# Attention outputs turned in 32 by 32 blocks by VectorE, and an output stage without TensorE transposes

## The chip, the cores and the metric

The kernel runs on one core of one Trainium2 chip. A core has a matrix engine (TensorE, in the profile PE for its matmuls and PEld for its weight loads), three engines that work on vectors (VectorE or DVE, ScalarE or ACT, GpSimd or POOL), and SyncE (SP), which in this kernel does nothing but issue DMAs, all in one queue and in the order of the program. Each engine works through its own instructions in order and waits on semaphores for the others. The metric is the device time of one execution in microseconds, lower is better; the number used is the median of three runs.

## The reference, cut to what matters

Two independent parts whose results stand side by side in the output:

```python
S, D, H, Dh, N, L = 2048, 576, 32, 18, 4, 512      # N segments of L rows

# part A: Infini-attention
q, k, v = (x @ w for w in (wq, wk, wv))            # split into 32 heads of 18
for s in range(N):
    p = softmax(q_s @ k_s.T * scale + causal_mask)  # within the segment
    a_dot = p @ v_s
    a_mem = (phi(q_s) @ M) / (phi(q_s) @ z + 1e-6)  # memory of the earlier segments
    o_s = g * a_mem + (1 - g) * a_dot               # g = sigmoid(beta), one per head
    M += phi(k_s).T @ v_s;  z += phi(k_s).sum(rows)
a = concat(o_s).reshape(S, D) @ wo

# part B: FNet mixing
b = dft_seq_re @ (x_b @ dft_hid_re.T) - dft_seq_im @ (x_b @ dft_hid_im.T)
return concatenate([a, b], axis=-1)                # S x 1152, float32
```

The change concerns the way of `o_s` to the product with `wo`. That product needs the attention output with the features (576 = 32 heads x 18) on the partitions, while attention produces it with the rows (positions) on the partitions, so that somewhere a transpose is needed.

## The kernel before, in words

The dense products run in three parts: each operand is split into a high part (rounded to the matmul's format) and a low rest, and hi*lo + hi*hi + lo*hi are added in PSUM.

**Stage 1, projections** (about 0 to 235 us). For each of the four segments, q, k and v are computed and written to DRAM (`qd`, `kd`, `vd`), and for segments 1 to 3 the memory term, already multiplied by g, is written by `lookup` as row tiles `amd[t]` of 128 x 576, t = 0..15 (L364, L365).

**Stage 2, attention woven into the dense FNet products** (about 235 to 950 us). Two generators run side by side. `dense()` gives the FNet matmuls in small pieces (`hidden`, `sequence`, L510 and L555 to L560). `attention()` (L826) walks over 64 steps p of two heads each, plus four steps in which the pipeline empties. Each step has eight slots with planned lengths (`SLOTS`); after each slot the main loop (L894) puts in as many dense matmuls as keep the two in proportion. The matmuls of attention are short and wait for other engines, those of `dense` wait for little, so that TensorE always has something to do. The order in which each engine gets its instructions is exactly the order in which this Python code runs. `later(n, f)` puts a call n slots later.

A group G is four heads; it takes two steps, 2G and 2G + 1, and there are 32 of them, eight per segment. In a step, `s_fill` (slots 0, 2, 3) computes scores of the even head for the row minima, which VectorE takes with a custom instruction (L691); `f_fill` (slots 4, 5, 6) does the same for the odd head of two steps earlier, whose exponentials ScalarE then takes (L714). Both take turns at two PSUM banks with the tag `s`: the matmul of `f_fill` kind 1 in slot 4 writes the bank whose scores of `s_fill` kind 1, slot 2, VectorE must have read. `t_lo` (L784) and `f_split_lo` (L725) are splits of the probabilities, partly on VectorE and partly on GpSimd; the odd head's probabilities are turned by a DMA transpose (L730). `pv` (L801, L802) multiplies with v.

Four steps after a step began its heads, in slot 7, `pv_out` (L804) normalises their output: a reciprocal, a product with 1 - g, a reduction over three parts (L816) and a product (L817) into the tile `og`, 128 partitions x 4 x 4 x 18, two buffers. After the second half of a group, `og` is written to `od[s][g8]` in DRAM (L820), with rows on the partitions and 4 x 72 features and row tiles in a row.

`y` (four buffers of 128 x 576) holds results of the dense products; in the second half of `dense` its tiles come back from DRAM (`y_load`), VectorE subtracts the PSUM result (L579), and the tile goes to the output's right half.

**Stage 3, output** (about 950 us to the end). For each of 16 row tiles, `o_load` fetches the eight group pieces of 128 x 72 and, for segments 1 to 3, the memory tile `amd[t]`; `o_join` adds the two on VectorE (L631) and copies the last 64 features twice (`otail`, L633); `o_transpose` turns five 128 x 128 blocks on TensorE (L644), and ScalarE and VectorE split the result from PSUM (L57, L649, L650). The main loop (L914) then runs two chains of 14 matmuls with the weights `wo` (28 per tile, L925 through the helper at L79), ScalarE takes the result out of PSUM (L926), and one DMA writes the tile (L930; in the last tile one for each half, L928). The loads for tile t + 2 are issued when tile t is transposed. The work for tile 0 starts about 3 us before the last dense matmul.

Of the kernel before, what the change touches and what calls it, by code (L numbers as in the profile page):

```python
# [38 lines left out]
def infini_attention_and_fnet(ctx: ExitStack, tc: tile.TileContext, xT, wqk, w8, wv, wo, beta, xtT, cT, hT, out):  # L39
# [10 lines left out]
    vd = [dram.tile([P, 4, 8, 220], BF16, name=f"vd{s}") for s in range(NSEG)]  # L50
    amd = [dram.tile([P, D], F32, name=f"amd{t}") for t in range(NT)]
    yd = [dram.tile([P, D], F32, name=f"yd{t}") for t in range(NT)]
    od = [dram.tile([8, P, 4, 72], F32, name=f"od{s}") for s in range(NSEG)]

# [28 lines left out]
    def later(n, fn, *a):  # L83
        due.setdefault(clock[0] + n, []).append((fn, a))
# [256 lines left out]
    def lookup(s, j):  # L341
# [22 lines left out]
        pool.tensor_tensor(am, nd[:, :, :DH], w.to_broadcast([P, H, DH]), OP.mult)  # L364
        later(1, dma, amd[4 * s + j], am.rearrange("p h d -> p (h d)"))  # L365
        yield
# [47 lines left out]

    CAUSAL, NEGM, MB = [], [], []

# [83 lines left out]
    def bank(name, shape, dtype, tag):  # L500
        turns[tag] ^= 1
        return ps.tile(shape, dtype, name=name, tag=f"{tag}{turns[tag]}", bufs=1)
# [34 lines left out]
    def y_load(tt):  # L537
        if tt < NT:
            Y[tt] = sb.tile([P, D], F32, name="y", bufs=4)
            dma(Y[tt], yd[tt])  # L540
# [26 lines left out]
    def sequence(ri, tt):  # L567
        if ri:
            y_load(tt + 1)
            y = Y.pop(tt)  # L570
        else:
            y = sb.tile([P, D], F32, name="y", bufs=4)

# [38 lines left out]
    O, O3, OT, WO, WORAW = {}, [], {}, [], []  # L612

    def o_load(t):
        if t >= NT:
            return
        s, j = divmod(t, 4)
        a = O3[0].tile([P, D], F32, name="o", bufs=3) if O3 else sb.tile([P, D], F32, name="raw", tag="raw", bufs=3)
        dma(a.rearrange("p (g c) -> p g c", g=8), od[s][:, :, j, :].rearrange("g p c -> p g c"))
        m = None  # L620
        if s:
            m = O3[0].tile([P, D], F32, name="oam", bufs=3)
            dma(m, amd[t])
        O[t] = a, m

    def o_join(t):
        if t >= NT:
            return
        a, m = O[t]
        if m is not None:  # L630
            dve.tensor_tensor(a, a, m, OP.add)  # L631
        tail = O3[0].tile([P, P], F32, name="otail", bufs=2)
        dve.tensor_copy(tail.rearrange("p (r c) -> p r c", r=2), a[:, None, 512:].to_broadcast([P, 2, 64]))  # L633
        O[t] = a, tail

    def o_transpose(t):
        if t >= NT:
            return
        o_load(t + 2)
        a, tail = O.pop(t)  # L640
        o = bank("ot", [P, 4, P], F32, "s")
        e = bank("ot1", [P, P], F32, "t")
        for c in range(5):
            pe.transpose(o[:, c] if c < 4 else e, a[:, c * P:(c + 1) * P] if c < 4 else tail, ident)  # L644
        hi = O3[0].tile([P, 4, P], F32R, name="oth", bufs=2)
        lo = O3[0].tile([P, 4, P], F32R, name="otl", bufs=2)
        tl = O3[0].tile([P, P], F32R, name="ott", bufs=2)
        split(hi, lo, o)
        act.activation(tl, e, AF.Copy)  # L649
        dve.tensor_tensor(tl[64:], e[64:], tl[64:].bitcast(F32), OP.subtract)  # L650
        OT[t] = hi, lo, tl
        o_join(t + 1)

# [15 lines left out]
    sa = p2a.enter_context(tc.tile_pool(name="sb2a", bufs=1, reuse_waits="tile"))  # L669
    PT, OG, PV = {}, {}, {}  # L670

# [132 lines left out]
    def pv_out(n2):  # L804
        G, hh = divmod(n2, 2)
        s, g8 = divmod(G, 8)
        o = PV.pop(n2)
        if hh == 0:
            OG[G] = sa.tile([P, 4, 4, DH], F32, name="og", bufs=2)
        h0 = 4 * g8 + 2 * hh  # L810
# [5 lines left out]
        dve.tensor_reduce(a, o[:, :, :, :54].rearrange("p h i (c d) -> p (h i) d c", c=3), axis=AX, op=OP.add)  # L816
        dve.tensor_tensor(OG[G][:, :, 2 * hh:2 * hh + 2, :].rearrange("p i h d -> p h i d"),  # L817
                          a.rearrange("p (h i) d -> p h i d", h=2), w.to_broadcast([P, 2, 4, DH]), OP.mult)
        if hh == 1:
            later(4, dma, od[s][g8], OG.pop(G).rearrange("p i h d -> p i (h d)"))  # L820

# [4 lines left out]
    def attention():  # L826
        for p in range(NP + V_LAG):
# [8 lines left out]
            if p < 2:  # L836
                stacks(sa, p + 2)
            if p == 0:
                value_load(0)
                stack_load(1)  # L840
            if p % 2 == 0:
                later(39, value_load, p // 2 + 1)
            if p == NP + 1:
                o_load(0)
                o_load(1)
# [59 lines left out]
    for t in d:  # L905
        tick()
        td += t or 0.0
        if 0 in O and td > total_d - 3000.0:
            o_join(0)
            o_transpose(0)  # L910
    while due:
        tick()

    for t in range(NT):  # L914
        o_transpose(t + 1)
        hi, lo, tl = OT.pop(t)
        y = O3[0].tile([P, D], F32, name="y3", bufs=2)
        for h in range(2):
# [7 lines left out]
            act.activation(y[:, cs], o, AF.Copy)  # L926
            if t == NT - 1:
                dma(out[t * P:, cs], y[:, cs])  # L928
        if t < NT - 1:
            dma(out[t * P:(t + 1) * P, :D], y)  # L930


_INS = ("xT", "wqk", "w8", "wv", "wo", "beta", "xtT", "cT", "hT")


# [28 lines left out]
```

## Time and profile before

| what | value |
|---|---|
| median of 3 runs | 1020.28 us (1017.42 to 1022.33) |
| the profiled execution: its time, its span | 1024.34 us, 1022.6 us |
| TensorE busy, matmuls | 1007.7 us (99%) |
| VectorE busy | 727.8 us (71%) |
| ScalarE busy | 711.4 us (70%) |
| GpSimd busy | 626.1 us (61%) |
| DMA | 208.39 MB, 297757 packets, mean 204 GB/s |

The profile is that of one execution. Busy shares are means over stages with different limits, so the stages have to be looked at by themselves. A row of a group of instructions gives the line, engine and operation, the tiles (written <- read), the shapes and the count, then after the bar the busy time in all and the mean of one in ns, then how long the engine stood idle just before them and what ended that. In the chain of work that ended last, each row has a start, a length, and the instruction. The timeline has start, length, engine, line, operation and tiles; an idle time before an instruction stands in brackets at the end of its row.

### The profile page before, as it was taken

The page shows a single profiled execution, that of the slowest core. Times are in us where ns is not written, and L with a number is a line of the kernel's source. Part 1 is how long each engine was busy: PE and PEld are TensorE (multiplying, and loading weights), DVE is VectorE, ACT ScalarE, POOL GpSimd, SP SyncE. Part 2 cuts the span into 40 slices and gives each one's busy share as a digit, 9 for nine tenths or more (in the row PEclk, how much of TensorE's full clock was granted, in tenths as well). Part 3 has the DMA queues.
Part 4 walks back from the last instruction along what each step waited for, and adds up shares of the span by engine and source line. Part 5 has one row for each costly group of instructions (what it writes and reads, how often), then busy time and mean ns, then how long its engine had stood idle before and what let it go on. Part 6 is the DMA issues. An engine that isn't in the chain of part 4 may idle for free.

```text
span 1022.6 us, 25516 instructions
## 1 busy us (share of the span) xinstructions
PE 1007.7 (99%) x9464; PEld 944.0 (92%) x9464; DVE 727.8 (71%) x1903; ACT 711.4 (70%) x1654; POOL 626.1 (61%) x668
## 2 busy tenths in 40 slices
PE   9999999989999999999999999999999999999998
PEld 8989989879999999999999999998999999999998
DVE  6645555555577777877888788887889888885442
ACT  7657475544687878787878788886768787875333
POOL 3557584775667676766775777666666676775000
PEclk9999999999999999999999999999999999999999
DMA  7538465677477989898898898688999999887574
GB/s 258 178 102 272 149 178 216 202 255 228 109 179 196 220 227 206 218 221 218 213 261 209 225 200 178 167 216 216 218 214 217 241 212 240 237 175 176 158 210 138
DMA packets 297757, 208.39 MB, mean 204 GB/s; under 512 B 208672, under 2 KB 250784, under 8 KB 297632
## 3 DMA queue, kind: packets, MB, share of 16 engines
q1 hardware_dynamic: 297632, 206.76, 77.4%
q8 instruction: 74, 1.21, 0.5%
q14 instruction: 51, 0.42, 0.1%
HBM read 120.80 MB, written 57.93 MB: 175 GB/s over the span
## 4 chain that ended last, share of the span: by engine, by line
PE 84%; DMA 4%; DVE 4%; ACT 3%; POOL 3%; issue 2%; POOLq 0%; SPq 0%; DVEq 0%; ACTq 0%
PE d L510 38%; PE s L685 7%; PE d L79 6%; PE pv L801 4%; PE qk L231 4%; PE qk L79 3%; PE d L555 3%; PE d L556 3%; PE d L557 3%; PE v L79 3%; PE pv L802 2%; PE t L759 1%; POOL p L268 1%; DMA amd<-am 1%; PE m L324 1%
## 5 line engine op out<-in xcount | busy, mean ns | idle before, releaser
L691 DVE CUSTOM_DVE_ANT_0 s<-s,causal 128x128 f32<-128x128 f32 (+3 forms) x512 | 250.4, 499 | 92.1 <-PE s L685 84.0
L403 POOL TENSOR_TENSOR clo<-craw,chi 128x512 fp32r<-128x512 f32 x158 | 212.0, 1342 | 103.1 <-ACT chi L398 71.7
L510 PE MATMUL d<-wide,chi 128*128 128x288 f32 x1408 | 266.7, 306 | 0.0
L510 PEld LDWEIGHTS d<-wide,chi 128*128 128x128 f32 x1408 | 212.4, 189 | 1.1
L510 PE MATMUL d<-wide,clo 128*128 128x288 f32 x704 | 178.1, 319 | 0.0
L725 POOL TENSOR_TENSOR hl<-pf,hl 128x768 f16<-128x768 f32 x64 | 116.1, 1814 | 71.9 <-ACT hl L721 64.2
L769 ACT ACTIVATE phi<-t 128x384 f16<-128x384 f32 x128 | 61.9, 484 | 105.6 <-PE t L766 105.5
L685 PE MATMUL s<-ks,qs 108*128 108x128 bf16 (+3 forms) x512 | 133.9, 304 | 1.2 <-DVE negm L691 1.0
L714 ACT ACTIVATE pf<-s,nb 128x128 f32<-128x128 f32 (+3 forms) x256 | 128.3, 527 | 6.2
L510 PE MATMUL d<-ab,chi 128*128 128x288 f32 x640 | 126.1, 306 | 0.0
L510 PEld LDWEIGHTS d<-wide,clo 128*128 128x128 f32 x704 | 119.1, 189 | 0.9
L784 DVE TENSOR_TENSOR plo<-pf,phi 128x384 f16<-128x384 f32 (+1 forms) x128 | 118.2, 923 | 0.0
L398 ACT ACTIVATE chi<-craw 128x512 fp32r<-128x512 f32 x160 | 100.4, 628 | 3.9 <-PE d L510 2.4
L770 ACT ACTIVATE pf<-t 128x384 f32<-128x384 f32 (+1 forms) x192 | 99.5, 518 | 3.3 <-PE t L759 3.2
L510 PEld LDWEIGHTS d<-ab,chi 128*128 128x128 f32 x640 | 98.6, 189 | 0.4
L721 ACT ACTIVATE hl<-pf 128x768 f16<-128x768 f32 (+1 forms) x128 | 87.4, 730 | 2.0
L510 PE MATMUL d<-ab,clo 128*128 128x288 f32 x320 | 85.0, 314 | 0.0
L555 PE MATMUL d<-wide,chi 128*128 128x288 f32 x256 | 84.1, 329 | 0.0
L725 DVE TENSOR_TENSOR hl<-pf,hl 128x512 f16<-128x512 f32 x64 | 76.6, 1198 | 0.2
L556 PE MATMUL d<-wide,chi 128*128 128x288 f32 x256 | 75.6, 295 | 0.0
L557 PE MATMUL d<-wide,clo 128*128 128x288 f32 x256 | 75.5, 295 | 0.0
L784 POOL TENSOR_TENSOR plo<-pf,phi 128x384 f16<-128x384 f32 x64 | 59.7, 933 | 18.7 <-ACT pf L770 15.9
(196 smaller groups left out, 2520.6 us busy)
## 6 DMA issues: line engine op xcount, KB each, us to landing
craw<-cT SPq DMA_DIRECT2D x128, 256.0 KB
ks<-kd SPq DMA_DIRECT2D x32, 432.0 KB
qs<-qd SPq DMA_DIRECT2D x32, 432.0 KB
craw<-xtT SPq DMA_DIRECT2D x32, 320.0 KB
out<-y SPq DMA_DIRECT2D x31, 288.0 KB
vd<-vs SPq DMA_DIRECT2D x16, 440.0 KB
vst<-vd SPq DMA_DIRECT2D x32, 220.0 KB
qd<-p SPq DMA_DIRECT2D x16, 384.0 KB
```

Of the source, the lines that this page charges most:

```text
L79: pe.matmul(o, a, b, start=n == 0, stop=n == len(terms) - 1)
L398: act.activation(hi, raw[:, :4], AF.Copy)
L403: engine.tensor_tensor(lo, raw[:, :4], hi.bitcast(F32), OP.subtract)
L510: pe.matmul(o[h], a, b[:, h * 288:h * 288 + 288], start=start, stop=stop)
L555: pe.matmul(o, xh[:, k], wl[k][:, cs], start=k == 0, stop=False)
L556: pe.matmul(o, xh[:, k], wh[k][:, cs], start=False, stop=False)
L557: pe.matmul(o, xl[:, k], wh[k][:, cs], start=False, stop=False)
L685: pe.matmul(o[:, c:c + w], q[:, i * P:w], k[:, :w], start=True, stop=True)
L691: dve.tensor_tensor_reduce(o[:, c:c + w], o[:, c:c + w], CAUSAL[0][:, L - w:], scale=scale, scalar=-LOWEST, op0=OP.add, op1=OP.min, accum_ ...
L714: act.activation(f[:, FIRST_COL[i]:FIRST_COL[i] + w], o[:, c:c + w], AF.Exp, bias=nb[:, i:i + 1], scale=-1.0)
L725: engine.tensor_tensor(hl[:, 1, a:b], f[:, a:b], hl[:, 0, a:b], OP.subtract)
L784: (pool if kind == 2 else dve).tensor_tensor(lo[:, a:b], f[:, a:b], hi[:, a:b], OP.subtract)
```

## The change

`pv_out` no longer leaves the output with rows on the partitions for TensorE to turn. Two persistent tiles `OG[0]`, `OG[1]` of 128 x 4 x 72 take turns by group. For segments 1 to 3, `memory_load` reads the group's memory term from `amd` (now one tile of 4 x 128 x 576 per segment) into `OG` ahead of `pv_out`, which adds its product to it. Two slots after the second half, `turn_out` transposes the first 64 of the group's 72 features in two VectorE instructions, each of which turns sixteen 32 x 32 blocks, and gathers the last 8 features of four groups in `ogl`, which is transposed once every four groups. Three slots later the results go to DRAM (`od`, `odt`), features first. The 32 x 32 blocks leave the features and the rows in a permuted order; the rows of `wo` are permuted to match on the host, and the output rows are put back by writing each tile with four DMAs of 32 rows (eight in the last tile). The output stage loads each tile already turned, in three DMAs, and splits it from SBUF; the TensorE transposes, the join and the copy of the tail are gone. `y` has three buffers in place of four.

```diff
--- before.py
+++ after.py
@@ -48,9 +48,10 @@
     qd = [dram.tile([D, 6, L], BF16, name=f"qd{s}") for s in range(NSEG)]
     kd = [dram.tile([D, 6, L], BF16, name=f"kd{s}") for s in range(NSEG)]
     vd = [dram.tile([P, 4, 8, 220], BF16, name=f"vd{s}") for s in range(NSEG)]
-    amd = [dram.tile([P, D], F32, name=f"amd{t}") for t in range(NT)]
+    amd = [dram.tile([4, P, D], F32, name=f"amd{s}") for s in range(NSEG)]
     yd = [dram.tile([P, D], F32, name=f"yd{t}") for t in range(NT)]
-    od = [dram.tile([8, P, 4, 72], F32, name=f"od{s}") for s in range(NSEG)]
+    od = [dram.tile([4, 4 * P, P], F32, name=f"od{s}") for s in range(NSEG)]
+    odt = [dram.tile([2 * P, P], F32, name=f"odt{s}") for s in range(NSEG)]
 
     def split(hi, lo, raw, lo_engine=None):
         act.activation(hi, raw, AF.Copy)
@@ -362,7 +363,7 @@
         dve.tensor_tensor(w, den, g[:, :, None], OP.mult)
         am = sb.tile([P, H, DH], F32, name="am", bufs=1)
         pool.tensor_tensor(am, nd[:, :, :DH], w.to_broadcast([P, H, DH]), OP.mult)
-        later(1, dma, amd[4 * s + j], am.rearrange("p h d -> p (h d)"))
+        later(1, dma, amd[s][j], am.rearrange("p h d -> p (h d)"))
         yield
 
     HW, HRAW = {}, {}
@@ -412,7 +413,7 @@
         ks_bufs.append(p_.tile([P, 4, L], BF16, name=f"ks{i}"))
         pool.memset(ks_bufs[i].bitcast(F32)[96:], BF16_ONES)
 
-    CAUSAL, NEGM, MB = [], [], []
+    CAUSAL, NEGM, MB, OG = [], [], [], []
 
     def attention_tiles():
         t = sr.tile([P, L], F32, name="causal")
@@ -536,7 +537,7 @@
 
     def y_load(tt):
         if tt < NT:
-            Y[tt] = sb.tile([P, D], F32, name="y", bufs=4)
+            Y[tt] = sb.tile([P, D], F32, name="y", bufs=3)
             dma(Y[tt], yd[tt])
 
     def chunk(n):
@@ -569,7 +570,7 @@
             y_load(tt + 1)
             y = Y.pop(tt)
         else:
-            y = sb.tile([P, D], F32, name="y", bufs=4)
+            y = sb.tile([P, D], F32, name="y", bufs=3)
 
         def evacuate(h, o):
             cs = slice(h * 288, h * 288 + 288)
@@ -611,45 +612,29 @@
 
     O, O3, OT, WO, WORAW = {}, [], {}, [], []
 
+
     def o_load(t):
         if t >= NT:
             return
-        s, j = divmod(t, 4)
-        a = O3[0].tile([P, D], F32, name="o", bufs=3) if O3 else sb.tile([P, D], F32, name="raw", tag="raw", bufs=3)
-        dma(a.rearrange("p (g c) -> p g c", g=8), od[s][:, :, j, :].rearrange("g p c -> p g c"))
-        m = None
-        if s:
-            m = O3[0].tile([P, D], F32, name="oam", bufs=3)
-            dma(m, amd[t])
-        O[t] = a, m
-
-    def o_join(t):
-        if t >= NT:
-            return
-        a, m = O[t]
-        if m is not None:
-            dve.tensor_tensor(a, a, m, OP.add)
-        tail = O3[0].tile([P, P], F32, name="otail", bufs=2)
-        dve.tensor_copy(tail.rearrange("p (r c) -> p r c", r=2), a[:, None, 512:].to_broadcast([P, 2, 64]))
-        O[t] = a, tail
-
-    def o_transpose(t):
+        s, a = divmod(t, 4)
+        o = O3[0].tile([P, 5, P], F32, name="o", bufs=3) if O3 else sb.tile([P, 5, P], F32, name="raw", tag="raw", bufs=3)
+        dma(o[:, :4], od[s][:, a * P:a * P + P].rearrange("c p x -> p c x"))
+        for i in range(2):
+            dma(o[64 * i:64 * i + 64, 4], odt[s][64 * a:64 * a + 64])
+        O[t] = o
+
+    def o_split(t):
         if t >= NT:
             return
         o_load(t + 2)
-        a, tail = O.pop(t)
-        o = bank("ot", [P, 4, P], F32, "s")
-        e = bank("ot1", [P, P], F32, "t")
-        for c in range(5):
-            pe.transpose(o[:, c] if c < 4 else e, a[:, c * P:(c + 1) * P] if c < 4 else tail, ident)
+        o = O.pop(t)
         hi = O3[0].tile([P, 4, P], F32R, name="oth", bufs=2)
         lo = O3[0].tile([P, 4, P], F32R, name="otl", bufs=2)
         tl = O3[0].tile([P, P], F32R, name="ott", bufs=2)
-        split(hi, lo, o)
-        act.activation(tl, e, AF.Copy)
-        dve.tensor_tensor(tl[64:], e[64:], tl[64:].bitcast(F32), OP.subtract)
+        split(hi, lo, o[:, :4])
+        act.activation(tl, o[:, 4], AF.Copy)
+        dve.tensor_tensor(tl[64:], o[64:, 4], tl[64:].bitcast(F32), OP.subtract)
         OT[t] = hi, lo, tl
-        o_join(t + 1)
 
     def wo_load(k):
         raw = sb.tile([P, D], F32, name="raw", tag="raw", bufs=3)
@@ -667,7 +652,7 @@
 
     p2a = ExitStack()
     sa = p2a.enter_context(tc.tile_pool(name="sb2a", bufs=1, reuse_waits="tile"))
-    PT, OG, PV = {}, {}, {}
+    PT, PV = {}, {}
 
 
 
@@ -805,8 +790,7 @@
         G, hh = divmod(n2, 2)
         s, g8 = divmod(G, 8)
         o = PV.pop(n2)
-        if hh == 0:
-            OG[G] = sa.tile([P, 4, 4, DH], F32, name="og", bufs=2)
+        og = OG[G % 2]
         h0 = 4 * g8 + 2 * hh
         w = o[:, 440:].rearrange("p (h i c) -> p h i c", h=2, c=1)
         o = o[:, :440].rearrange("p (h i c) -> p h i c", h=2, i=4)
@@ -814,10 +798,42 @@
         dve.reciprocal(w, o[:, :, :, 54:])
         dve.tensor_tensor(w, w, g1[:, h0:h0 + 2, None, None].to_broadcast([P, 2, 4, 1]), OP.mult)
         dve.tensor_reduce(a, o[:, :, :, :54].rearrange("p h i (c d) -> p (h i) d c", c=3), axis=AX, op=OP.add)
-        dve.tensor_tensor(OG[G][:, :, 2 * hh:2 * hh + 2, :].rearrange("p i h d -> p h i d"),
-                          a.rearrange("p (h i) d -> p h i d", h=2), w.to_broadcast([P, 2, 4, DH]), OP.mult)
+        to = og[:, :, 36 * hh:36 * hh + 36].rearrange("p i (h d) -> p h i d", d=DH)
+        a = a.rearrange("p (h i) d -> p h i d", h=2)
+        if s == 0:
+            dve.tensor_tensor(to, a, w.to_broadcast([P, 2, 4, DH]), OP.mult)
+        else:
+            dve.tensor_tensor(a, a, w.to_broadcast([P, 2, 4, DH]), OP.mult)
+            dve.tensor_tensor(to, to, a, OP.add)
         if hh == 1:
-            later(4, dma, od[s][g8], OG.pop(G).rearrange("p i h d -> p i (h d)"))
+            later(2, turn_out, G)
+
+
+
+    TAILS = []
+
+    def turn_out(G):
+        s, g8 = divmod(G, 8)
+        og = OG[G % 2]
+        t = sa.tile([P, 2, 4, 32], F32, name="ogt", bufs=1)
+        for b in range(2):
+            dve.transpose(t[:, b], og[:, :, 32 * b:32 * b + 32])
+        later(3, dma, od[s][g8 // 2].rearrange("(p u) x -> p (u x)", u=4)[:, 256 * (g8 % 2):256 * (g8 % 2) + 256],
+              t.rearrange("p b q j -> p (b q j)"))
+        if G % 4 == 0:
+            TAILS.append(sa.tile([P, 4, 32], F32, name="ogl", bufs=1))
+        l = TAILS[-1]
+        dve.tensor_copy(l[:, :, 8 * (G % 4):8 * (G % 4) + 8], og[:, :, 64:])
+        if G % 4 == 3:
+            t = sa.tile([P, 4, 32], F32, name="oglt", bufs=1)
+            dve.transpose(t, l)
+            u = g8 // 4
+            later(3, dma, odt[s].rearrange("(p u) x -> p u x", u=2)[:, u], t.rearrange("p q j -> p (q j)"))
+
+    def memory_load(G):
+        if 8 <= G < NG:
+            s, g8 = divmod(G, 8)
+            dma(OG[G % 2], amd[s][:, :, 72 * g8:72 * g8 + 72].rearrange("q p c -> p q c"))
 
     F_LAG, T_LAG, V_LAG = 2, 3, 4
     NP = 2 * NG
@@ -835,11 +851,13 @@
 
             if p < 2:
                 stacks(sa, p + 2)
+                OG.append(sa.tile([P, 4, 72], F32, name=f"og{p}"))
             if p == 0:
                 value_load(0)
                 stack_load(1)
             if p % 2 == 0:
                 later(39, value_load, p // 2 + 1)
+                later(30, memory_load, p // 2)
             if p == NP + 1:
                 o_load(0)
                 o_load(1)
@@ -906,13 +924,12 @@
         tick()
         td += t or 0.0
         if 0 in O and td > total_d - 3000.0:
-            o_join(0)
-            o_transpose(0)
+            o_split(0)
     while due:
         tick()
 
     for t in range(NT):
-        o_transpose(t + 1)
+        o_split(t + 1)
         hi, lo, tl = OT.pop(t)
         y = O3[0].tile([P, D], F32, name="y3", bufs=2)
         for h in range(2):
@@ -924,13 +941,22 @@
                 terms += [(hi[:, k], wl[k][:, cs]), (hi[:, k], wh[k][:, cs]), (lo[:, k], wh[k][:, cs])]
             chain(o, terms + [(tl, wt1[:, cs]), (tl, wt2[:, cs])])
             act.activation(y[:, cs], o, AF.Copy)
-            if t == NT - 1:
-                dma(out[t * P:, cs], y[:, cs])
-        if t < NT - 1:
-            dma(out[t * P:(t + 1) * P, :D], y)
+            if h or t == NT - 1:
+                cs = cs if t == NT - 1 else slice(0, D)
+                for q in range(4):
+                    r = 512 * (t // 4) + P * q + 32 * (t % 4)
+                    dma(out[r:r + 32, cs], y[32 * q:32 * q + 32, cs])
 
 
 _INS = ("xT", "wqk", "w8", "wv", "wo", "beta", "xtT", "cT", "hT")
+
+
+def _out_features():
+
+
+    f = np.arange(D).reshape(8, 72)
+    main = f[:, :64].reshape(4, 4, 32).transpose(0, 2, 1)
+    return np.concatenate([main.ravel(), f[:, 64:].reshape(2, 32).T.ravel()])
 
 
 def _tail_twice(a):
@@ -945,7 +971,7 @@
         "wqk": _tail_twice(np.concatenate([wq[:, :512], wk[:, :512]], axis=1)),
         "w8": _tail_twice(np.concatenate([wq[:, 512:], wk[:, 512:]], axis=1)).transpose(1, 0, 2).reshape(P, 5 * P),
         "wv": _tail_twice(wv),
-        "wo": _tail_twice(wo),
+        "wo": _tail_twice(wo[_out_features()]),
         "beta": np.asarray(A_beta),
         "xtT": _tail_twice(np.asarray(B_x)[0].T).reshape(5, P, NT, P).transpose(2, 1, 0, 3),
         "cT": c.reshape(2, NT, P, 4, 4, P).transpose(0, 1, 3, 5, 4, 2),
```

## The prediction

> **What bounds the kernel now.** I read the page's head and busy times first, then the chain of waits, then windows by stage.
>
> ```profile
> span 1022.6 us, 25516 instructions
> PE 1007.7 (99%) x9464; PEld 944.0 (92%) x9464; DVE 727.8 (71%) x1903; ACT 711.4 (70%) x1654; POOL 626.1 (61%) x668
> PE 84%; DMA 4%; DVE 4%; ACT 3%; POOL 3%; issue 2%; POOLq 0%; SPq 0%; DVEq 0%; ACTq 0%
> ```
>
> TensorE is busy throughout, and 84% of the chain that ended last is its own work. The windows say whether others have room (columns: window, length, busy time of PE, PEld, DVE, ACT and POOL with counts, granted clock, DMA share, GB/s):
>
> ```profile
> 230.00:950.00 720.00, 716.08 (x7555) 674.31 (x7556) 570.14 (x1597) 545.56 (x1302) 487.09 (x515) 1.00 0.85 207
> 800.00:900.00 100.00, 99.61 (x1093) 93.23 (x1093) 85.50 (x239) 76.59 (x177) 70.22 (x72) 1.00 0.95 228
> ```
>
> In attention TensorE stands still for some 4 of 720 us, at a full granted clock. VectorE has 14.5 us left in 100, the DMA engines show a share of 0.95: what is moved into this stage costs nothing only while it doesn't make TensorE wait. The waits of the whole run show how close that is:
>
> ```profile
> PE trm L742 <- DVE og L817: 2.2, 5, 0.9
> PE s L685 <- DVE negm L691: 1.0, 2, 0.7
> DVE s L691 <- PE s L685: 84.0, 123, 2.0
> ```
>
> TensorE waits 3.2 us for VectorE, VectorE 84 us for scores. The end of the chain, in order of time (start, length):
>
> ```profile
> 949.50 0.55 PE ot L644 x5
> ...
> 951.92 0.55 PE ot L644 x5
> 952.46 3.71 PE d L79 x28
> ...
> 1011.46 0.55 PE ot L644 x5
> 1012.01 7.43 PE d L79 x56
> ```
>
> The output stage is TensorE without a gap: 28 matmuls in 3.71 us, five transposes in 0.545 us (951.92 to 952.46, 1011.46 to 1012.01), and the next tile.
>
> **The change part by part.**
>
> *Transposes off TensorE: a gain of 8.7 us.* All 16 groups of five lie on the chain: 16 x 0.545 = 8.72. What could be late next, at a tile every 3.71 us in place of 4.25?
>
> ```profile
> L56 ACT ACTIVATE oth<-ot 128x512 fp32r<-128x512 f32 x16 | 9.6, 599 | 11.0 <-PE ot L644 10.6
> L649 ACT ACTIVATE ott<-ot 128x128 fp32r<-128x128 f32 x16 | 4.4, 272 | 0.0
> L926 ACT ACTIVATE y<-d 128x288 f32<-128x288 f32 x32 | 13.2, 412 | 42.5 <-PE d L79 26.4 <-issue 16.0
> L57 DVE TENSOR_TENSOR otl<-ot,oth 128x512 fp32r<-128x512 f32 x16 | 11.1, 692 | 34.5 <-ACT oth L56 34.5
> L631 DVE TENSOR_TENSOR o<-o,oam 128x576 f32<-128x576 f32 x12 | 9.1, 759 | 0.4
> L633 DVE COPY otail<-o 128x128 f32<-128x128 f32 x14 | 3.2, 226 | 0.5
> ```
>
> ScalarE needs 0.60 + 0.27 + 2 x 0.41 = 1.69 us a tile, VectorE 0.69 us and a quarter of it again for its two splits; both fit. The next tile's high part can start when the last copy out of PSUM is done, 0.4 us into the chain, and its low part ends some 2 us into it (0.41 + 0.60 + 0.69 and a hand-over). The splits read SBUF now; even 20% dearer they fit. The join and the tail copy (9.1 + 3.2 us of VectorE) vanish from a stage where VectorE waits: worth nothing.
>
> *SP's queue in the output stage.* Three loads and four stores a tile replace two loads and one store.
>
> ```profile
> 1003.43 0.34 SPq L930 DMA_DIRECT2D out<-y  x1
> 1003.87 0.37 SPq L619 DMA_DIRECT2D o<-od  x1
> 1004.30 0.70 SPq L623 DMA_DIRECT2D oam<-amd  x1
> ```
>
> From start to start an issue takes 0.43 to 0.44 us, and 0.70 plus a gap behind a load of many pieces. Seven: 6 x 0.44 + 0.75 = 3.4 us of 3.71. It fits, barely. The stores wait for the tile's last copy, and the loads for four tiles on are queued behind them; those have two more tiles, 7.4 us, until they are needed. Bytes fall from three times 128 x 576 x 4 (288 KB each) to 608 KB a tile. So: nothing, with a bound of its own among the rivals.
>
> *The last tile's stores: a loss of 1.2 us.* Its second half leaves in four DMAs, not one, three more issues behind the last copy: 3 x 0.43 = 1.3 us; smaller pieces land a little sooner. Bounds: nothing (if the landing is what takes time, and overlaps) and 2.1 (at 0.70 each). I take 1.2, near the stores' own spacing.
>
> *VectorE's added work in attention.* For each group: two transposes of 128 x 128; a copy of 128 x 32; a quarter of one more transpose; and for segments 1 to 3 an add of 128 x 144 in each half. No row shows a VectorE transpose. Nearest rows: the copy of as many elements, 226 ns (L633), and the instruction of 128 x 128 with two inputs, 307 ns:
>
> ```profile
> L691 DVE CUSTOM_DVE_ANT_0 s<-s,causal 128x128 f32<-128x128 f32 x128 | 39.3, 307 | 41.6 <-PE s L685 38.8 <-ACT pf L770 1.9 <-ACT y L577 0.6
> L817 DVE TENSOR_TENSOR og<-pa,pv 128x144 f32<-128x144 f32 x64 | 19.4, 304 | 2.2
> ```
>
> I take 300 (bounds 226, and 600 if it moved four bytes in two passes). The Trainium skill (VectorE: DVE Perf Modes, The three transpose paths) gives 311 ns for 128 x 128 in bf16; with that the sum would be the same. The bunch that ends a group is then 0.30 (second add, as the product in L817) + 2 x 0.30 + 0.15 (the copy: a quarter of the elements of the 226 ns one) + 0.08 = 1.13 us. It falls where VectorE often waits: `turn_out` comes behind the scores of slot 0 and ahead of those of slot 2, the 128 x 128 row above, with 41.6 us idle before it. In the timeline a step with room, then one without:
>
> ```profile
> 811.43 0.14 DVE L691 DVE_READ_ACCUMULATOR2_ANT negm<- 128x1 f32 x1
> 812.70 0.46 DVE L579 TENSOR_TENSOR y<-y,d 128x288 f32<-128x288 f32 x1 [1.14 <-PE d L510]
> ...
> 728.91 2.16 DVE L784 TENSOR_TENSOR plo<-pf,phi 128x512 f16<-128x512 f32 x1
> 730.99 0.69 DVE L691 CUSTOM_DVE_ANT_0 s<-s,causal 128x512 f32<-128x512 f32 x1
> 731.60 0.33 DVE L691 CUSTOM_DVE_ANT_0 s<-s,causal 128x128 f32<-128x128 f32 x1
> 732.01 0.57 DVE L691 CUSTOM_DVE_ANT_0 s<-s,causal 128x384 f32<-128x384 f32 x1
> ...
> 733.06 0.39 PE L685 MATMUL s<-ks,qs 108*128 108x128 bf16 x2
> ```
>
> At 812 nearly the whole bunch goes into 1.14 us of waiting. At 731 there is none. Queued behind the bunch are the scores of slot 2, and the matmul at 733.06 needs their bank, free at 732.58: 0.48 us of slack, 0.37 after the 0.1 that a hand-over takes. There the bunch costs 1.13 - 0.37 = 0.76 us of TensorE. I went through the 29 even steps from 306 to 894 us in this way: seven have less room than the bunch, the first behind the scores at 431.69, the last behind those at 853.05, and their shortfalls add up to 3.8 us (2.6 with a bunch of 0.95, 7.2 with one of 1.46):
>
> ```profile
> 431.69 0.69 DVE L691 CUSTOM_DVE_ANT_0 s<-s,causal 128x512 f32<-128x512 f32 x1
> 853.05 0.69 DVE L691 CUSTOM_DVE_ANT_0 s<-s,causal 128x512 f32<-128x512 f32 x1
> ```
>
> I take 3.8. The first half's add, alone in its step, fits into the room. The transpose of the maxima, which waits for `pv_out`, reads its bank free before the add, so that wait stays.
>
> *Loads and stores moved into attention: nothing.* 24 `memory_load`s of 144 KB (128 x 4 x 72 x 4 bytes) are 3.5 MB, over 24 of the stage's 34 group times, some 500 us, 7 GB/s beside 207; `od` is written in as many bytes as before. A load in 512 pieces holds SP for about 0.59 us:
>
> ```profile
> L441 SPq DMA_DIRECT2D vst<-vd x32: 584/591/1244, 242.9 to 920.2; - x32
> 804.57 3.72 SPq L730 DMA_TRANSPOSE ptt<-hl  x1
> 808.35 0.54 SPq L89 DMA_DIRECT2D ks<-kd  x1
> 819.95 0.30 DVE L817 TENSOR_TENSOR og<-pa,pv 128x144 f32<-128x144 f32 x1
> ```
>
> It is issued where the `ks` load at 808.35 stands, behind a DMA transpose, and is needed by the add behind 819.95: 11.6 us. `ks` and `qs` slip by 0.6 us and serve the group after next. The stores move behind the transposes by a slot; if VectorE is late, SP waits there with the next step's loads behind it. The third `y` buffer is free: a load takes the one stored two products earlier.
>
> *Sum* against the profiled execution, 1024.34 us (span 1022.6 plus 1.7 around it): -8.7 + 1.2 + 3.8 = -3.7, 1020.6 us. That execution lies 4.1 us above the median of the three runs, 1020.28; from the median the same difference gives **1016.6 us**.
>
> **Rivals.**
>
> *The room holds throughout.* The bunch is shorter or falls into waits: at most 1 us lost, 1020.28 - 8.7 + 1.2 + 0.5 = 1013.3. For it: VectorE's 84 us of waits. Against: the steps like 731.
>
> *VectorE is held and becomes the bound: slower.* The 2.16 us at 728.91 is work with a median of 0.69 over both its shapes: it waits while GpSimd runs. The new add reads two SBUF tiles at this very place, so it can be held in its turn, and the split behind it again, by GpSimd instructions as long as these:
>
> ```profile
> L784 DVE TENSOR_TENSOR plo<-pf,phi x128: 552/686/2169, 278.6 to 940.3; 128x384 f16<-128x384 f32 x64, 128x512 f16<-128x512 f32 x64
> L403 POOL TENSOR_TENSOR clo<-craw,chi 128x512 fp32r<-128x512 f32 x158 | 212.0, 1342 | 103.1 <-ACT chi L398 71.7 <-ACT nb L711 16.6 <-POOL plo L784 3.5
> ```
>
> One hold of 1.34 makes the bunch 2.47 us. With 2.2 the same count over the steps gives 20 us: 1020.28 - 7.5 + 20 = 1033; with 1.8, 12.7 us: 1025.5, from where it is slower by over 0.5%. A transpose of 600 ns makes the bunch 1.8 by itself. For it: GpSimd is busy 70% of the time at 800. Against: VectorE has 14.5 us in 100 left, 1.5 in a step of 10.6, and what holds the add spares the split. The Trainium skill (SBUF — State Buffer, Who interferes with whom) states that a VectorE instruction with two SBUF inputs and a GpSimd instruction that reads SBUF shut each other out for a whole instruction; the 2.16 us agrees, and by that rule this rival gains.
>
> *SP bounds the output stage.* At 0.59 us an issue, seven take 4.13 us, 0.42 over a tile's matmuls: 16 x 0.42 = 6.7 us, 1023. From 0.53 us on it decides. Against: the stores' 0.34.
>
> *Memory loads or DMA transposes land late* at a share of 0.95: 24 groups x 0.3 us = 7, about 1024.
>
> **How the numbers follow.** Chances: the forecast, 1014 to 1019.5, 0.36; room throughout, 1011 to 1014, 0.26; VectorE held, 1021 to 1035, 0.26; SP 0.07; late landings 0.05. About 0.5%, 5.1 us, is what a measurement tells from no change. Faster by more (below 1015.2): all of the second case, 0.14 of the first, 0.40; slower (above 1025.4): 0.20 of the third, 0.04 of the last two, 0.24; between, 0.36. The range 1010.5 to 1029 leaves out the end of the third case, about 0.12, and a little below. The forecast's own is 1014 to 1019.5.
>
> **What would show it.** In the profile after: no transposes in the output stage, tiles 3.71 us apart (longer: SP or a load); VectorE transposes of about 0.3 us; waits of TensorE's scores for VectorE grown from 1.0 to about 5 us (20: the held add; unchanged: the room held); the last store 1.2 us later behind the last matmul. Wrong it would be through transposes of twice the price, an add of over 1 us, or a tile of more than 4 us.

## The result, and the profile after

The changed kernel takes 1036.82 us (median of 4 runs, 1032.87 to 1038.68) against 1021.31 before; the ratio is 1.0145, 95% interval 1.0121 to 1.0170. It is slower by about 15 us, where a gain of 3.7 was forecast, and lies above the end of the range (1029). Ratios and intervals here and below are taken over all runs of two kernels and are not quotients of the medians shown.

The profiled execution after took 1038.45 us. Parts of its page, the window of attention with the same columns as before, and the end of the chain of waits:

```profile
span 1036.7 us, 25628 instructions
PE 1005.1 (97%) x9384; PEld 937.6 (90%) x9384; DVE 773.7 (75%) x2027; ACT 711.4 (69%) x1654; POOL 625.8 (60%) x668
PE 67%; DVE 17%; issue 4%; DMA 4%; ACT 4%; POOL 3%; SPq 1%; POOLq 0%; DVEq 0%; ACTq 0%
```

```profile
230.00:950.00 720.00, 700.47 (x7306) 655.72 (x7305) 613.44 (x1709) 535.76 (x1277) 474.71 (x507) 1.00 0.85 207
```

```profile
968.58 4.33 PE d L511 x32
972.90 59.42 PE d L80 x448
1032.32 0.02 issue
1032.35 0.41 ACT y L943
```

Put beside the rows of before, three stretches account for the whole difference of 14.1 us between the spans. The output stage begins at 972.90, not 952.46: +20.4. Its 16 tiles, one after the other without a gap, take 59.42 us, where they took 66.98 (952.46 to 1019.44): -7.6. From the last matmul to the end of the span pass 4.4 us, not 3.2: +1.2. Two of the sixteen groups of transposes, 1.1 us, lay ahead of 952.46, so the stages ahead of the output grew by 21.5 us. Attention itself grew by a little more, 23.2 us: its first dense matmul started at 235.7 us, before at 237.4. VectorE was on 4% of the chain, and is on 17% of it now. In the window of 720 us, TensorE lost 15.6 us against 716.08 before, and VectorE is busy for 43 more, at the same mean clock and the same DMA share.

The waits of TensorE, and the groups of VectorE's instructions that the change added, with the row that showed the room:

```profile
PE s L670 <- DVE negm L676: 11.5, 17, 1.7
PE trm L727 <- DVE pa L806: 3.3, 5, 0.9
PE v L80 <- DVE vr L305: 3.1, 1, 3.1
PE pv L787 <- DVE plo L769: 2.1, 5, 1.0
```

```profile
L807 DVE TENSOR_TENSOR og<-og,pa 128x144 f32<-128x144 f32 x48 | 42.8, 892 | 1.7
L826 DVE COPY ogl<-og 128x32 f32<-128x32 f32 x32 | 19.4, 608 | 0.0
L820 DVE STREAM_TRANSPOSE ogt<-og 128x128 f32<-128x128 f32 x64 | 15.8, 283 | 0.0
L676 DVE CUSTOM_DVE_ANT_0 s<-s,causal 128x128 f32<-128x128 f32 x128 | 39.3, 307 | 17.4 <-PE s L670 15.8 <-ACT pf L755 1.1
```

The transposes cost 283 ns, about the 300 that were taken for them. The add costs 892 ns a piece in place of 304, and the small tail copy 608 in place of 150. The room ahead of the scores of slot 2 shrank from 41.6 to 17.4 us, and TensorE's waits for VectorE at the scores grew from 1.0 to 11.5. One step in the timelines, VectorE first, then GpSimd:

```profile
952.81 0.30 DVE L806 TENSOR_TENSOR pa<-pa,pv 128x144 f32<-128x144 f32 x1
953.15 1.82 DVE L807 TENSOR_TENSOR og<-og,pa 128x144 f32<-128x144 f32 x1
954.89 1.77 DVE L769 TENSOR_TENSOR plo<-pf,phi 128x512 f16<-128x512 f32 x1
956.59 0.49 DVE L820 STREAM_TRANSPOSE ogt<-og 128x128 f32<-128x128 f32 x2
957.01 0.18 DVE L826 COPY ogl<-og 128x32 f32<-128x32 f32 x1
```

```profile
953.14 1.67 POOL L710 TENSOR_TENSOR hl<-pf,hl 128x768 f16<-128x768 f32 x1 [1.92 <-ACT hl L706]
954.75 1.36 POOL L404 TENSOR_TENSOR clo<-craw,chi 128x512 fp32r<-128x512 f32 x1
956.07 1.08 POOL L759 TENSOR_SCALAR_AFFINE_SELECT pf<-pf 128x512 f32<-128x512 f32 x1
```

GpSimd's split starts at 953.14, the add 10 ns later. The add ends at 954.97, 0.16 us behind the split; then GpSimd has its next split running, and VectorE's own split ends only 0.5 us behind that one. The add has not taken the hold off the split that follows it: both are held, one after the other, and some 2.6 us of VectorE are gone (1.82 - 0.30 and 1.77 - 0.69).

The timelines of all 48 adds and 32 tail copies show the same. 29 adds took 0.37 us or more. At the start of each of them a GpSimd instruction was running, and each ended 0.15 to 0.18 us after that one did. The other 19 took 0.31 us; they began while GpSimd stood idle or was within 0.06 us of an end. Of the copies 26 were held, and each ended 0.03 to 0.05 us behind GpSimd. Half of the first halves' adds are among the held ones (mean 0.75 us, second halves 1.04).

In one place the two holds cost more than a wait. At 766.88 an add was held for 1.81 us and the split behind it for 1.77, a subtraction (L580) came late, and TensorE stood still for it; in the stretch after that its granted clock was 0.60 (the columns of the second row: window, length, TensorE's busy time, clock, DMA share, GB/s):

```profile
771.41 0.53 PE L511 MATMUL d<-wide,chi 128*128 128x288 f32 x2 [1.71 <-DVE y L580]
772.00:776.00 4.00, 4.00 (x39) 0.60 0.60 150
```

Worked out from these rows, that is 1.7 us of waiting and 4 x 0.40 = 1.6 us of lost clock. The same wait, of 1.7 and 2.2 us with a fall of the clock behind it, stands in no_turn and turn_later below; where it was 0.8 us or less (tail_copy_act, stand_in, add_from_psum) no fall shows. That the wait causes it was not tested.

### The profile page after: what moved, and what is told of

It reads as the page before. It is cut to its first block, busy times and chain, and to the rows that moved or that the text cites. A ratio compares the mean times of both kernels' runs of the same rounds, so it can differ in the third digit from the quotient of the medians.

```text
span 1036.7 us, 25628 instructions
## 1 busy us (share of the span) xinstructions
PE 1005.1 (97%) x9384; PEld 937.6 (90%) x9384; DVE 773.7 (75%) x2027; ACT 711.4 (69%) x1654; POOL 625.8 (60%) x668
## 4 chain that ended last, share of the span: by engine, by line
PE 67%; DVE 17%; issue 4%; DMA 4%; ACT 4%; POOL 3%; SPq 1%; POOLq 0%; DVEq 0%; ACTq 0%
PE d L511 27%; PE s L670 6%; PE d L80 6%; PE qk L232 4%; DVE plo L769 4%; DVE s L676 4%; PE pv L786 3%; PE qk L80 3%; PE v L80 3%; PE d L556 2%; PE d L557 2%; PE d L558 2%; DVE og L807 2%; PE pv L787 2%; DVE pa L800 2%
## 5 line engine op out<-in xcount | busy, mean ns | idle before, releaser
L670 PE MATMUL s<-ks,qs 108*128 108x128 bf16 (+3 forms) x512 | 134.1, 304 | 12.0 <-DVE negm L676 11.5
L769 DVE TENSOR_TENSOR plo<-pf,phi 128x384 f16<-128x384 f32 (+1 forms) x128 | 123.4, 964 | 0.0
L670 PEld LDWEIGHTS <-qs 108*128 108x128 bf16 x512 | 41.6, 98 | 32.1 <-issue 13.4
```

Of the source, the lines that this page charges most:

```text
L670: pe.matmul(o[:, c:c + w], q[:, i * P:w], k[:, :w], start=True, stop=True)
L769: (pool if kind == 2 else dve).tensor_tensor(lo[:, a:b], f[:, a:b], hi[:, a:b], OP.subtract)
```

## The experiments

Three theories for what was lost in attention. An instruction is called held here when it runs longer than its own work takes and ends with a GpSimd instruction. **H**: the added instructions are held by GpSimd's, and that is most of the loss. **W**: any added work on VectorE costs at this place, held or not, in proportion to its time. **M**: the memory loads moved into attention, and the DMA queue behind them, are the loss.

| kernel | median, us | ratio to before | interval |
|---|---|---|---|
| the change | 1036.82 | 1.0145 | 1.0121 to 1.0170 |
| out_stage_only | 1014.72 | 0.9936 | 0.9922 to 0.9951 |
| no_add | 1018.33 | 0.9979 | 0.9955 to 1.0002 |
| no_turn | 1025.57 | 1.0032 | 1.0015 to 1.0049 |
| add_from_psum | 1027.53 | 1.0063 | 1.0046 to 1.0079 |
| tail_copy_act | 1024.59 | 1.0037 | 1.0019 to 1.0055 |
| stand_in | 1023.73 | 1.0022 | 1.0005 to 1.0039 |
| turn_later | 1032.58 | 1.0101 | 1.0078 to 1.0125 |
| add_on_gpsimd | 1017.81 | 0.9957 | 0.9942 to 0.9973 |
| gpsimd_and_act | 1015.85 | 0.9956 | 0.9938 to 0.9973 |
| two_queues | 1015.32 | 0.9927 | 0.9906 to 0.9947 |

The medians are of 4 to 10 runs, and the kernel before had medians of 1021.3 to 1022.8 us beside them. The runs of one kernel lie up to 9 us apart (no_add: 1015.91 to 1024.78), and the intervals reach 1.5 to 2.5 us to either side, so a difference of under some 3 us between two kernels is not told from none.

**The output stage alone**

```diff
-            dve.tensor_tensor(a, a, w.to_broadcast([P, 2, 4, DH]), OP.mult)
-            dve.tensor_tensor(to, to, a, OP.add)
+            dve.tensor_tensor(to, a, w.to_broadcast([P, 2, 4, DH]), OP.mult)
...
-        for b in range(2):
-            dve.transpose(t[:, b], og[:, :, 32 * b:32 * b + 32])
...
-        dve.tensor_copy(l[:, :, 8 * (G % 4):8 * (G % 4) + 8], og[:, :, 64:])
...
+        flat = og.rearrange("p q c -> p (q c)")
+        later(3, dma, od[s][g8 // 2].rearrange("(p u) x -> p (u x)", u=4)[:, 256 * (g8 % 2):256 * (g8 % 2) + 256], flat[:, :256])
+        if G % 4 == 3:
+            u = g8 // 4
+            later(3, dma, odt[s].rearrange("(p u) x -> p u x", u=2)[:, u], flat[:, 160:])
...
-                later(30, memory_load, p // 2)
```

> The changed kernel with attention's added VectorE work taken out: no memory load, no add, no transposes, no tail copy; the untransposed tile goes to od and odt in stores of the same sizes. Leaves out: the memory term and the turning, so the output's left half is not the reference's. All theories that put the loss into the added work of attention: 1021.3 - 8.7 (transposes off TensorE) + 1.2 (last stores) = 1013.8 us, attention as long as before (output stage begins near 951 us). If the output stage, the three y buffers or the stores cost something by themselves: more than 1018.

1014.72: 6.7 us under the before of its runs, against 7.5 worked out. The output stage, the three stores and one load a tile more in SP's queue, the loss of the fourth `y` buffer and the wider tiles cost nothing that shows. Everything that was lost, 1036.8 - 1014.7 = 22.1 us, lies in what this kernel leaves out.

**Without the add**

```diff
-            dve.tensor_tensor(a, a, w.to_broadcast([P, 2, 4, DH]), OP.mult)
-            dve.tensor_tensor(to, to, a, OP.add)
+            dve.tensor_tensor(to, a, w.to_broadcast([P, 2, 4, DH]), OP.mult)
```

> The changed kernel without the add of the memory term (the product overwrites the loaded tile, as segment 0 does); loads, transposes and tail copy stay. Leaves out: the memory term. Theory H (the add with two SBUF inputs is held by GpSimd, and that is most of the loss): 1013.8 + about 5 = 1019 us. Theory W (every us of VectorE work there costs the same; add 42 us of 77 added): 1013.8 + 9.8 + 0 = 1023.6. Theory M (the memory loads in the DMA queue are the loss): 1036, unchanged.

1018.33. M falls: the 24 loads and all stores are in this kernel. Transposes, tail copy and loads together cost 3.6 us over the output stage alone; with the add come the other 18.5, nearly as H had it. Its waits at the scores are nearly those of before:

```profile
PE trm L727 <- DVE og L806: 1.8, 4, 0.9
PE s L670 <- DVE negm L676: 1.8, 5, 0.7
```

**Without the turning**

```diff
-        t = sa.tile([P, 2, 4, 32], F32, name="ogt", bufs=1)
-        for b in range(2):
-            dve.transpose(t[:, b], og[:, :, 32 * b:32 * b + 32])
...
-        dve.tensor_copy(l[:, :, 8 * (G % 4):8 * (G % 4) + 8], og[:, :, 64:])
...
+        flat = og.rearrange("p q c -> p (q c)")
+        later(3, dma, od[s][g8 // 2].rearrange("(p u) x -> p (u x)", u=4)[:, 256 * (g8 % 2):256 * (g8 % 2) + 256], flat[:, :256])
...
```

> The changed kernel without transposes and tail copy, add and memory loads kept; the untransposed tile is stored. Leaves out: the turning, so the left half is not the reference's. H: most of the loss stays, about 1030 us, the add's mean still 0.9 us. W: 1013.8 + 42/77 x 21.5 = 1025.5. M: 1036.

1025.57, as W had it by proportion, though the same proportion missed no_add by 5.3 us; H expected more. The adds, still held (a mean of 801 ns), cost 10.9 us by themselves. With the 3.6 us of the turning that makes 14.5, but both together cost 22.1. The difference, 7.6 us, is clear of the noise (by the four intervals some 4 us to either side): the two parts make each other dearer.

**The add with one operand in PSUM**

```diff
-        o = PV.pop(n2)
+        o = PVRAW[n2] = PV.pop(n2)
...
-            dve.tensor_tensor(a, a, w.to_broadcast([P, 2, 4, DH]), OP.mult)
-            dve.tensor_tensor(to, to, a, OP.add)
+            m = PVRAW.pop(n2)[:, :144].rearrange("p (h i d) -> p h i d", h=2, i=4)
+            dve.tensor_tensor(m, a, w.to_broadcast([P, 2, 4, DH]), OP.mult)
+            dve.tensor_tensor(to, to, m, OP.add)
```

> The changed kernel with one operand changed: the product of pv_out goes to PSUM (into the bank that the reduction has read), and the add takes it from there, so that it has one SBUF input. Same work, same result. H: the add's mean falls from 917 to about 305 ns, and the time to 1020 to 1023 us. W: VectorE busy falls by 28 us of 77, so to about 1028. M: 1036.

The same work, with the place of one operand changed. The add's row in the changed kernel, then here (minimum, median and maximum in ns):

```profile
L807 DVE TENSOR_TENSOR og<-og,pa x48: 307/596/1823, 457.9 to 970.1; 128x144 f32<-128x144 f32 x48
```

```profile
L808 DVE TENSOR_TENSOR og<-og,pv x48: 303/303/306, 455.9 to 956.6; 128x144 f32<-128x144 f32 x48
```

Not one of the 48 is held any more, and 9.3 us come back, although 28 of them start while GpSimd is running an instruction (29 in the changed kernel). So the second operand in SBUF lets GpSimd hold the add. But at 1027.53 the kernel remains 9.2 us above no_add, more than H left room for. W's figure is hit by luck: it took VectorE's busy time to fall by 28 us, and it fell by 14.6 (773.7 to 759.1). The adds did get 28 us shorter in all, but part of the hold moved on to instructions behind them: VectorE's two splits of 128x512 went from a mean of 1068 and 975 ns to 1177 and 1049, which is 11.6 us over the run.

**A stand-in for the add's work**

```diff
-            dve.tensor_tensor(a, a, w.to_broadcast([P, 2, 4, DH]), OP.mult)
-            dve.tensor_tensor(to, to, a, OP.add)
+            dve.tensor_tensor(to, a, w.to_broadcast([P, 2, 4, DH]), OP.mult)
+            dve.transpose(sa.tile([P, 4, 32], F32, name="scratch", bufs=1), og[:, :, :32])
```

> The changed kernel with a VectorE transpose of 128x128 into a scratch tile (one SBUF input, 283 ns, never held) in the place of each add. Leaves out: the memory term. Tells the work of an add apart from its hold and from the longer use of the PSUM bank in add_from_psum (1027.5). W: as long as add_from_psum, 1027. H with a price on the bank: 1020 to 1023. If the hold is all: as no_add, 1018.

1023.73: 48 instructions of 308 ns, none of them held, with the PSUM bank freed as early as in the change, cost 5.4 us over no_add. So added work that isn't held itself costs too, as W says. The split behind it is held longer than in no_add (a mean of 1156 against 1003 ns). The 3.8 us from here to add_from_psum go with the longer use of the PSUM bank there, though no run takes that alone: in add_from_psum the transpose of the maxima waits 5.8 us for the bank that the add still reads, in the stand-in 3.0. The waits of add_from_psum:

```profile
PE s L670 <- DVE negm L676: 6.2, 10, 1.2
PE trm L727 <- DVE og L808: 5.8, 8, 1.3
```

**The tail copy on ScalarE**

```diff
-        dve.tensor_copy(l[:, :, 8 * (G % 4):8 * (G % 4) + 8], og[:, :, 64:])
+        act.activation(l[:, :, 8 * (G % 4):8 * (G % 4) + 8], og[:, :, 64:], AF.Copy)
```

> The changed kernel with the tail copy (608 ns a piece on VectorE, 32 times) on ScalarE. H (held instructions are the loss): VectorE loses 19 us of held time per run at the bunch; as no_turn against the change shows 11 us for transposes and copy together (19.4 us the copy, 18 us the transposes), about 6 us gone: 1031. W (only unheld work counts, 32 x 0.13): under 2 us gone, 1035.

12 us come back, twice what H expected, for a copy of 32 elements per partition that has 130 ns of work where nothing holds it:

```profile
L826 DVE COPY ogl<-og x32: 130/602/1430, 305.8 to 970.7; 128x32 f32<-128x32 f32 x32
```

It stands last in the bunch (but for one transpose in every fourth group), right ahead of the scores that TensorE waits for, once in each group. On ScalarE it takes 219 ns, and the adds are held less than in the change (a mean of 774 against 892 ns). The kernel is now as fast as no_turn, which leaves the transposes out as well (1024.59 and 1025.57). So beside the add it is the tail copy that makes the turning dear, and the transposes cost nothing that shows.

**The turning one step later**

```diff
-            later(2, turn_out, G)
+            later(10, turn_out, G)
```

> The changed kernel with one number changed: turn_out 10 slots behind pv_out, not 2, so that the transposes and the tail copy fall into the step after the add, not behind it. Same work, same holds. If the sum of the two in one step is what makes them dear (no_turn and no_add alone cost 10.9 and 3.6 us over the output stage alone, together 22.1): 1014.7 + 10.9 + 3.6 = 1029. If only the amount counts: 1036, unchanged.

1032.58, a ratio of 1.0101: about 4 us better than the change, where 8 were expected. But the edit doesn't part the add and the turning. `pv_out` runs in every step, so ten slots behind the second half of one group the turning stands behind the add of the next group's first half, at the same distance (in the trace an add at 602.67, the transposes at 604.48). What changed is which add it follows: the first halves' adds take 0.66 us on average in this kernel, the second halves' 0.96. So why the two cost more together stays open.

**The add on GpSimd, and both moves together**

```diff
-            dve.tensor_tensor(to, to, a, OP.add)
+            pool.tensor_tensor(to, to, a, OP.add)
...
-            later(2, turn_out, G)
+            later(10, turn_out, G)
```

> The changed kernel with the add on GpSimd and turn_out 10 slots, not 2, behind pv_out, so that VectorE doesn't wait for it. H and W: VectorE is as in no_add, 1018 to 1020 us, if GpSimd has the room (67% busy); if GpSimd becomes the late one (its splits feed the DMA transposes): above 1024. M: 1036.

> Both at once: add on GpSimd, tail copy on ScalarE. VectorE keeps two and a quarter transposes a group. H: 1014.7 (output stage alone) + 1 to 2 us = 1016. W: 18 us of 77 VectorE work left: 1018 to 1019.

Both kernels have the turning ten slots behind, as in the run before. 1017.81, as no_add within the scatter; with the tail copy on ScalarE besides (the edit shown above), 1015.85. In the second, the waits for scores are those of the kernel before (1.0 us), and the room is back at 40.6 us, though two and a quarter transposes a group are still on VectorE:

```profile
PE trm L727 <- DVE pa L806: 3.7, 5, 1.2
PE s L670 <- DVE negm L676: 1.0, 2, 0.7
```

```profile
L676 DVE CUSTOM_DVE_ANT_0 s<-s,causal 128x128 f32<-128x128 f32 x128 | 39.0, 305 | 40.6 <-PE s L670 39.0 <-ACT chi L399 0.6 <-ACT ogl L826 0.5
L820 DVE STREAM_TRANSPOSE ogt<-og 128x128 f32<-128x128 f32 x64 | 16.1, 287 | 0.4 <-POOL og L807 0.4
L807 POOL TENSOR_TENSOR og<-og,pa 128x144 f32<-128x144 f32 x48 | 36.6, 762 | 94.8 <-DVE pa L806 89.4 <-DMA ptt<-hl 2.5 <-DMA og<-amd 1.8
```

GpSimd has the room: 36.6 us in attention, and ahead of its adds it stands idle, mostly for VectorE's product. The split of VectorE behind the add, which was held in the kernel before as well, is shorter here too (128x512: a mean of 741 ns against 1013).

**The last stores from two queues**

```diff
-                    dma(out[r:r + 32, cs], y[32 * q:32 * q + 32, cs])
+                    (nc.scalar.dma_start if t == NT - 1 and q % 2 else dma)(out[r:r + 32, cs], y[32 * q:32 * q + 32, cs])
```

> gpsimd_and_act (1015.85) with every second store of the last tile issued from ScalarE's queue in place of SP's. The last store is issued two places earlier, 2 x 0.46 us, and ScalarE's issues start behind its own copy: from the last matmul's end to the end of the span 4.6 us in gpsimd_and_act, 3.8 here, so 1015.0 us; if an issue from ScalarE takes longer than one from SP, unchanged.

```profile
1010.31 0.02 issue
1010.33 0.41 ACT y L943
```

From 1010.31, the end of the last matmul, to the end of the span, 1013.9, pass 3.6 us, close to the 3.8 worked out; in gpsimd_and_act it was 4.6. The median, 1015.32, cannot be told from that of gpsimd_and_act, but against the kernel before it is faster: 0.9927, 0.9906 to 0.9947, some 7 us. This version is faster than the kernel before and than the change.

## Why the prediction was wrong

*TensorE's side was right.* -8.7 and +1.2 add up to -7.5; the output stage alone gave -6.7 between medians, and the three stretches of the chain -7.6, -1.1 (the two groups ahead of it) and +1.2. Tiles came 59.42 / 16 = 3.71 us apart, as said.

*"VectorE's added work in attention: I take 3.8" is the step that failed;* it was 22.1 us. The step has three faults.

First, the bunch of 1.13 us was put together from durations of instructions that nothing holds: 0.30 for the add, from a product with one operand in PSUM, and 0.15 for the tail copy, from a copy in the output stage, where GpSimd does nothing. They measured 0.89 and 0.61. The transposes, the one price for which there was no row, were right. The hold stood among the rivals, with the right mechanism, for the add only and with a chance of 0.26; the split at 728.91, 2.16 us long, was the evidence for it, at the very place to which the add was moved. The argument against it, "what holds the add spares the split", holds for a small part only: in the changed kernel the splits of 128x512 took 1068 ns on average, no less than the 1013 before, and at 953 GpSimd has its next instruction ready and holds the split in its turn; with the add from PSUM they took 1177. A rival with its cause in a quoted row should have been the forecast. By the Trainium skill (SBUF — State Buffer, Who interferes with whom) a VectorE copy is one of the operations that can take the port pair shared with GpSimd, and so can be held by it like an add with two SBUF inputs. The 130 to 1430 ns agree, and the prediction weighed that rule for the add alone.

Second, the slack was counted bank by bank for one wait, that of slot 4 for slot 2, and step by step as if each began afresh. With a bunch of 1.13 us that gave 3.8 (counted again in the same seven steps by the same rule, it comes nearer to 5), and the adds of the first halves were said to fit into the room. Half of those were held. In six of the seven steps the split stands at 1.55 to 2.17 us, so the steps without room were just those in which GpSimd holds VectorE. The stand-in shows that even 48 unheld instructions, on top of the turning, cost 5.4 us. TensorE's wait for the transpose of the maxima, said to stay, grew from 2.2 to 3.7 us.

Third, the shortfalls of single steps were added up, and costs don't add here: the two parts cost 3.6 and 10.9 us apart, 22.1 together. The same shows per microsecond of VectorE. Turning and tail copy alone, some 42 us of its time, cost 3.6; the adds alone, 38, cost 10.9; but taking the tail copy off the full kernel, 19 us, gave back 12. Why later microseconds cost more was not shown.

*SP's queue* was called barely fitting, 3.4 of 3.71 us a tile. In the timeline of its issues after the change it is full:

```profile
987.31 0.38 SPq L621 DMA_DIRECT2D o<-od  x1
987.73 1.20 SPq L623 DMA_DIRECT2D o<-odt  x2
989.03 1.93 SPq L948 DMA_DIRECT2D out<-y  x4
991.06 0.39 SPq L621 DMA_DIRECT2D o<-od  x1
```

From 987.31 to 991.06 are 3.75 us without a pause, the four stores at 0.48 each, not 0.44: a little more than TensorE's 3.71. Over ten tiles, from 983.54 to 1023.22, the loads come 3.97 us apart, a part of it waiting for ScalarE's copies, so the queue falls behind TensorE. The chain shows no gap in sixteen tiles because they start with two tiles loaded ahead; that was a hair, not a margin.

*Memory loads: nothing* was right: gpsimd_and_act has all of them and lies 1.1 us above the output stage alone. *Late DMA landings* did not show: TensorE's waits name no DMA.

## What to carry to other kernels

Before work is moved to an engine that "has room", look in the trace at the longest, not the mean, of the instructions that already stand at that place: a maximum of three times the median, as here 2.17 us against 0.69, says that something holds them. It may hold the newcomer as well: here it held the add and the copy, and never the transposes. Price an added VectorE instruction by whether it reads two inputs from SBUF or copies SBUF to SBUF beside a busy GpSimd. Moving it to ScalarE or to GpSimd itself can be worth more than its own work: 12 us for 32 copies of 0.13 us. An operand in PSUM frees the instruction of the hold, but part of the hold passes to the next one. And on an engine near its limit do not add costs up: run the parts alone and together.

## What the runs showed of the hardware that was not expected

A VectorE copy of 128 x 32 float32 from SBUF to SBUF took 130 ns at the least and 1430 at the most, with a mean of 608 beside a GpSimd that is busy two thirds of the time in attention. The hold lasts until GpSimd's instruction ends, however little the held instruction has to do: 26 copies ended 0.03 to 0.05 us behind it. An add of 128 x 144 with both inputs in SBUF took 307 to 1823 ns, and with one in PSUM 303 to 306 on all 48. A VectorE transpose of sixteen 32 x 32 float32 blocks took 260 to 313 ns, about as long as an unheld add of nearly as many elements, and was never held: in the stand-in one that began 0.01 us behind a GpSimd split of 1.66 us took 0.31. On SP, a store of 32 rows held the queue for about 0.48 us when four followed each other; the one store of 128 rows a tile in the kernel before took 0.34.
